# A retention block and an MLP mixer on one core: seven products of quarters in all batches, masked products by copy and select, a tabled order

## The chip, the cores and the metric

The kernel runs on one core of one Trainium2 chip. The metric is the device time of one execution in microseconds. Before: 205.49 us, the median of 3 runs (204.29 to 206.15). The engines are named as in the profile: PE (matrix products), PEld (its weight loads), DVE, ACT and POOL (elementwise work; POOL also issues most loads), SP (issues DMA transposes).

## What is computed

```python
# q, k, v: (4, 8, 768, 64) float32; 8 heads of 64 make 512 columns
gamma = 1.0 - 2.0 ** (-5.0 - np.arange(H))
for t in range(S):
    state = gamma * state + np.einsum('bhd,bhe->bhde', k[:, :, t], v[:, :, t])
    y[:, :, t] = scale * np.einsum('bhd,bhde->bhe', q[:, :, t], state)
x = y.transpose(0, 2, 1, 3).reshape(B, S, H * D)         # (4, 768, 512)
h = np.maximum(x.T @ w_tok1, 0.0) @ w_tok2                # mixes 768 tokens through 256
u = x + h.T
out = u + np.maximum(u @ w_ch1, 0.0) @ w_ch2              # 512 -> 1536 -> 512
```

The inputs are float32; the products are made in float16 with sums in float32.

## The kernel before, in words

The sequence is cut into 6 chunks of 128 rows. A *front* does one pair of heads of one batch (4 batches x 4 pairs = 16 fronts): it loads q, k and v (cast to float16 by the load), scales k by powers of gamma (L491 on ACT, L493 on DVE or POOL), turns q and k so that the head dimension lies on partitions (`turn`: on PE with a copy by ACT or DVE, L525 and L535, or by a DMA transpose from SP, L514), makes the chunk products k'v (L550), the running states on DVE (L560, L562) and their scaled copy `r` (L574, L576), the scores of each chunk (L595), which DVE multiplies by a mask that holds the causal zeros and the powers of gamma (`am`, L609), and the result (L623, L626). ACT scales it into X (L639) or DVE does (L643); X is cast to float16 (L656); two token products follow (L667 with a relu on ACT at L682, then L731), DVE adds them into X (L738); the sum is cast (L746) and turned into `uT`, on PE (L765, L771) or by a DMA transpose (L755).

A *back* does one batch: `widen` makes relu(u @ w_ch1) for one half of the rows, 12 blocks of 128 columns, 4 products of 128x384 each (L800, relu on ACT at L816). Then either `narrow`, for each block of 128 rows 12 products of 512 columns (L839), added to X by DVE (L852) and stored; or `narrow7`, which takes two row blocks and cuts the product into quarters: seven products of quarters instead of eight. For two row blocks that is 42 products of 256 columns (L908) instead of 24 of 512. It needs four sums of pieces of `h` on DVE (L881), one copy on ACT (L944) and eleven quarter adds on DVE (L928), and sums of the weights made once (L1022). `SEVEN = (2, 3)` names the batches that use it; the last two row blocks of batch 3 use `narrow`.

The order of the work is planned when the program is built. Every step is an `Op` with a priority, the engines that may do it with a cost each, the steps it depends on, and the buffers it takes and uses. `arrange` plays the list through a model of the engines and of the DMA rings and gives each engine its order; within an engine the program then runs strictly in that order. Before, the rank of a step comes from its priority: constants first, then batch 0, then fronts at the places named in `PLACES` among the parts of the backs. Loads are issued on POOL in the order of `ORDER`, each behind the one before it (`request`), and each needs a free buffer (`BUFS`). The first k load goes through SP in float32 (`HARD`) and is cast by ACT (L501).

While the plan has PE idle for more than 400 ns in its first 21 us, the program puts products on a tile of zeros there (L1044):

```python
if o.start < F_ON and o.start - pe_at > 400:
    for _ in range(int((o.start - pe_at) * FILL / F_NS)):
        nc.tensor.matmul(spare[:, :384], zero[:, :P], zero, start=True, stop=True)
```

These fillers are not steps of the plan. They read `zero`, which is set by a step of the plan on DVE:

```python
zero_op = prep("DVE", 260, lambda: nc.vector.memset(zero, 0.0))
```

Other constants made on DVE at the start: the powers `lgs`, `gp`, the identity `ident16`, eight masks (L387), the scalings `gyw` (L1014) and zeros in `r16`.

## Time and profile before

| | |
|---|---|
| runs (3) | median 205.49 us, 204.29 to 206.15 |
| the profiled execution | 206.47 us, its span 204.6 us, mean granted clock 0.982 |
| busy, share of the span | PE 92%, PEld 63%, DVE 66%, ACT 51%, POOL 49% |
| chain that ended last | PE 50%, DMA 33%, POOL 7%, DVE 4%, issue 3% |
| DMA | 107991 packets, 26.27 MB; queue of POOL 13.18 MB, of SP 6.49 MB, of ACT 6.29 MB |

The page divides the span into 40 slices and gives busy tenths of each engine; its groups give line, engine, operation, count, busy time, mean duration, and what ended the idle time before. A matmul's duration is from its start to its modelled end, so that neighbours overlap; the spacing of starts tells what one costs.

### The profile page before, as it was taken

To read this page: it belongs to the slowest core of one execution; us is meant where nothing else is said; L and a number is where in the kernel's file an instruction comes from. 1 tells how busy PE (TensorE), PEld (TensorE's weight loads), DVE (VectorE), ACT (ScalarE), POOL (GpSimd) and SP (SyncE) were. 2 spreads that over 40 slices of the span, in tenths; PEclk is the share of its full clock that TensorE was granted. 3 is DMA by queue.
4 is the path that set the end of the run, shared out by engine and by line. 5 is a ranking of instruction groups with operands and counts; after the bars stand their busy time and mean duration, and the time that the engine had idled before them with its cause. 6 is when DMAs were issued, how large, how long until landed. Compare 5 with 4: busy or idle time off the path is not lost.

```text
span 204.6 us, 4851 instructions
## 1 busy us (share of the span) xinstructions
PE 187.8 (92%) x1907; PEld 128.1 (63%) x1907; DVE 135.8 (66%) x346; ACT 105.1 (51%) x234; POOL 99.8 (49%) x141
## 2 busy tenths in 40 slices
PE   7958898999897899999899979799999999999992
PEld 3536687575654555576557745466777886667861
DVE  7998889265988584769559536666732996044951
ACT  4576686885856350676134732086766003774000
POOL 8979598766867774627774864072340000000000
PEclk9995799999999999999999999999999999999999
DMA  9999999999999999999999999972011132000132
GB/s 115 147 156 171 191 179 161 137 200 131 179 126 151 189 152 192 187 173 151 125 180 185 156 150 139 174 175 59 4 38 38 44 153 112 6 0 0 62 147 103
DMA packets 107991, 26.27 MB, mean 128 GB/s; under 512 B 100161, under 2 KB 105025, under 8 KB 107969
## 3 DMA queue, kind: packets, MB, share of 16 engines
q0 software_dynamic: 78016, 13.18, 92.8%
q1 hardware_dynamic: 26352, 6.49, 26.2%
q10 hardware_dynamic: 3600, 6.29, 10.0%
q8 instruction: 15, 0.25, 0.5%
q14 instruction: 8, 0.06, 0.1%
HBM read 26.74 MB, written 6.29 MB: 161 GB/s over the span
## 4 chain that ended last, share of the span: by engine, by line
PE 50%; DMA 33%; POOL 7%; DVE 4%; issue 3%; ACT 1%; POOLq 0%; DVEq 0%
PE bank L800 16%; DMA v<-in_v_dram 14%; PE bank L908 11%; PE bank L839 10%; DMA qT<-q 9%; DMA wc<-in_moe_w_ch_dram 7%; DMA q<-in_q_dram 4%; PE bank L731 3%; PE bank L667 3%; POOL v L440 2%; PE bank L626 2%; DVE X L738 2%; PE bank L595 2%; PE bank L525 2%; PE bank L623 1%
## 5 line engine op out<-in xcount | busy, mean ns | idle before, releaser
L800 PE MATMUL bank<-uT,wc 128*128 128x384 f16 x384 | 69.0, 326 | 0.0
L816 ACT ACTIVATE h<-bank 128x384 f16<-128x384 f32 x96 | 46.4, 491 | 20.5 <-PE bank L800 20.0
L800 PEld LDWEIGHTS <-wc 128*128 128x128 f16 x384 | 35.5, 98 | 20.8
L839 PE MATMUL bank<-wc,h 128*128 128x512 f16 (+1 forms) x180 | 40.8, 365 | 0.0
L609 DVE TENSOR_TENSOR am<-bank,mask 128x384 f16<-128x384 f32 x64 | 32.4, 548 | 10.2 <-PE bank L595 10.2
L639 ACT ACTIVATE X<-bank,gy 128x192 f32<-128x192 f32 x58 | 21.1, 419 | 21.8 <-PE bank L626 19.8
L839 PEld LDWEIGHTS <-h 128*128 128x128 f16 x180 | 16.2, 98 | 13.3
L738 DVE TENSOR_TENSOR X<-X,bank 128x384 f32<-128x384 f32 x32 | 16.4, 549 | 12.0 <-PE bank L731 11.9
L562 DVE SCALAR_TENSOR_TENSOR U<-U,gp,bank 128x128 f32<-128x128 f32 x64 | 22.0, 343 | 1.9
L746 POOL CAST u<-X 128x384 f16<-128x384 f32 x26 | 13.5, 534 | 18.7 <-DVE X L738 17.1
L438 POOL DMA_DIRECT2D k<-in_k_dram x24 | 19.9, 838 | 3.4 <-DMA v<-in_v_dram 1.3
L440 POOL DMA_DIRECT2D v<-in_v_dram x16 | 16.6, 1035 | 6.6 <-DMA wc<-in_moe_w_ch_dram 1.9
L656 POOL CAST x<-X 128x384 f16<-128x384 f32 x21 | 11.3, 538 | 14.6 <-ACT X L639 14.3
L852 DVE TENSOR_TENSOR X<-X,bank 128x512 f32<-128x512 f32 (+1 forms) x15 | 9.7, 649 | 10.9 <-PE bank L839 10.9
L667 PE MATMUL bank<-x,wt 128*128 128x128 f16 x192 | 13.8, 219 | 2.6 <-POOL x L656 2.5
L626 PEld LDWEIGHTS <-am 128*128 128x128 f16 x192 | 13.1, 100 | 4.1 <-issue 1.4
L626 PE MATMUL bank<-v,am 128*128 128x64 f16 x192 | 14.7, 196 | 0.9 <-DVE am L609 0.9
L881 DVE TENSOR_TENSOR hs<-h 128x768 f16<-128x768 f16 x8 | 4.4, 552 | 16.5 <-ACT h L816 16.5
L667 PEld LDWEIGHTS <-wt 128*128 128x128 f16 x192 | 12.0, 98 | 5.0 <-issue 2.9
L731 PE MATMUL bank<-h,wt 128*128 128x128 f16 x192 | 13.5, 219 | 0.5 <-ACT h L682 0.5
L438 POOL DMA_DIRECT2D q<-in_q_dram x16 | 13.4, 840 | 1.2 <-DMA k<-in_k_dram 1.0
L731 PEld LDWEIGHTS <-wt 128*128 128x128 f16 x192 | 11.9, 98 | 2.8 <-issue 0.6
(70 smaller groups left out, 258.3 us busy)
## 6 DMA issues: line engine op xcount, KB each, us to landing
out_dram<-X ACTq DMA_DIRECT2D x23, 256.0 KB, 3.1
v<-in_v_dram POOLq DMA_DIRECT2D x16, 192.0 KB, 11.0
wc<-in_moe_w_ch_dram POOLq DMA_DIRECT2D x5, 512.0 KB, 12.7
k<-in_k_dram POOLq DMA_DIRECT2D x24, 96.0 KB, 11.2
q<-in_q_dram POOLq DMA_DIRECT2D x8, 192.0 KB, 9.4
q<-in_q_dram POOLq DMA_DIRECT2D x16, 96.0 KB, 10.7
wt<-in_moe_w_tok_dram POOLq DMA_DIRECT2D x2, 384.0 KB, 9.9
k<-in_k_dram POOLq DMA_DIRECT2D x3, 192.0 KB, 6.8
```

The costliest lines, as they stand in the source:

```text
L438: nc.gpsimd.dma_start(out=t[:, :, j], in_=src[j].rearrange("(c p) d -> p c d", p=P))
L440: nc.gpsimd.dma_start(out=tile_of(s, [P, 2, NC, D], F16), in_=src.rearrange("h (c p) d -> p (h c) d", p=P))
L562: nc.vector.scalar_tensor_tensor(out=u[:, c], in0=u[:, c - 1], scalar=gp[:, p:p + 1], in1=st, op0=ALU.mult, op1=ALU.add)
L609: nc.vector.tensor_tensor(am, src, m, ALU.mult)
L626: nc.tensor.matmul(o[:, j * D:(j + 1) * D], AM[2 * hf + j].tile[:, i], V.tile[:, j, c], start=(c == 0), stop=(c == 0 or j == 1))
L639: nc.scalar.mul(X.tile[:, half(hf), h * D:(h + 1) * D], yv[:, :, j * D:(j + 1) * D], gy[:, h:h + 1])
L667: nc.tensor.matmul(acc[:, jt * P:(jt + 1) * P], wt1[:, i, jt * P:(jt + 1) * P], X16.tile[:, i], start=(i == 0), stop=(i == NC - 1))
L731: nc.tensor.matmul(acc[:, i * P:(i + 1) * P], wt2[:, jt, t], H1.tile[:, jt], start=(jt == 0), stop=(jt == NJ - 1))
L800: nc.tensor.matmul(acc[:, :SH], w[:, ct, (ft % FW) * P:(ft % FW + 1) * P], UT.tile[:, ct, sh * SH:(sh + 1) * SH], start=(ct == 0), stop=(c ...
L816: nc.scalar.activation(H2.tile[:, ft], A.tile[:, :SH], AF.Relu)
L839: nc.tensor.matmul(acc, H2.tile[:, ft, i * P:(i + 1) * P], wc2[:, ft, cols], start=(ft == 0), stop=(ft == NF - 1 and not mixed))
L908: nc.tensor.matmul(acc[:, half], l[:, j], r[:, j], start=(j == 0), stop=(j == K2 - 1 and not more))
```

## The change

1. `SEVEN` names all four batches: the row blocks of batches 0 and 1, made by `narrow` before, go through `narrow7`.
2. In batches 1 to 3 the masked products of the second head of each pair (24 of 64) are made by a copy on ACT and a select in place on POOL. For that the mask holds only zeros and ones, and one mask serves all heads.
3. The powers of gamma reach the scores through k: the scaled k is what is turned. The extra cast of the first k is dropped; all k loads are one DMA of both heads. k is turned on PE in batch 1 too (`TURNS`), in whole chunks of 128 columns also in batch 0.
4. `BUFS` of k and v go from 5 to 4. The model's constants change, as do `PLACES` and `ORDER`.
5. The rank of each step comes from a table of 1,220 two-character numbers, `PRECEDENCE`, instead of its priority. It covers all steps, constants included.

```diff
--- before.py
+++ after.py
@@ -43,10 +43,12 @@
 
     GEN = dict(SP=20.0, POOL=8.0, ACT=20.0)
     FIRST = dict(SP=600, POOL=1300, ACT=700)
-    LAND = dict(SP=900, POOL=1600, ACT=1500)
+    LAND = dict(SP=900, POOL=1900, ACT=2000)
     DT = 40.0
-    MIX = 9.0
-    WAIT = 2500
+    MIX = 8.0
+    WAIT = 4000
+    SLOW = 1.03
+    PAD = 1500
 
     def __init__(self):
         self.t = 0.0
@@ -69,6 +71,8 @@
         on = [(q, l[0]) for q, l in self.line.items() if l and l[0][2] <= t]
         if on:
             round_ = sum(x[0].dma[1] for _, x in on) + self.MIX * (len(on) - 1)
+            if t > 25000:
+                round_ *= self.SLOW
             for q, x in on:
                 n = dt / round_
                 if x[3] > t:
@@ -76,7 +80,7 @@
                 x[1] -= n
                 if x[1] <= 0:
                     self.line[q].pop(0)
-                    landed.append((x[0], t + dt + self.LAND[q] + x[4]))
+                    landed.append((x[0], t + dt + self.LAND[q] + x[4] + (self.PAD if t > 25000 else 0)))
         self.t = t + dt
 
 
@@ -182,13 +186,9 @@
                 wake = min(wake, free[e])
                 continue
             w_ = waiting[e]
-            look = 0
             for o in w_:
                 if begun[o.n]:
                     continue
-                look += 1
-                if look > (1 if fixed is not None else 400):
-                    break
                 r = ready(o, e)
                 if r > t:
                     if r < INF:
@@ -204,7 +204,7 @@
                 else:
                     way = None
                     for w in o.ways:
-                        f = max(t, free[w[0]]) + w[2] + (400 if w[0] == "DVE" and t > 30000 else 300 if w[0] == "DVE" else 0)
+                        f = max(t, free[w[0]]) + w[2] + (800 if w[0] == "DVE" and t > 30000 else 300 if w[0] == "DVE" else 0)
                         if way is None or f < way[0] or (f == way[0] and w[0] == e):
                             way = (f, w)
                     if way[1][0] != e:
@@ -258,6 +258,34 @@
     return max(x for x in end), order, start, end
 
 
+
+PRECEDENCE = (
+    "xsldqatllmu0r37erv3xst5jcadieq4rs6123y25t201xhauk5mvkyp9gbl86jqki5djlf3rkxe4rsr49p88tuf7gafl4c0qmenxl4x1tra8"
...
+    "b217bgbamj5u97omgvliormp90khljfd20d5bu9q6ul7dappxota93f1s3ip4qkz"
+)
+
+
 @with_exitstack
 def tile_retnet_recurrent__then__mlp_mixer_token_channel_kernel(
     ctx: ExitStack,
@@ -291,19 +319,22 @@
     ps = ctx.enter_context(tc.tile_pool(name="ps", bufs=1, space=bass.MemoryType.PSUM))
     ctx.enter_context(tc.manual_schedule())
 
-    BUFS = dict(kf=1, k=5, q=4, v=5, k16=3, kT=4, qT=4, U=2, r16=3, am=8, X=3, x16=4, h1=5, u16=3,
+    BUFS = dict(kf=1, k=4, q=4, v=4, k16=3, kT=4, qT=4, U=2, r16=3, am=8, X=3, x16=4, h1=5, u16=3,
                 uT=2, h2=2, hs=2, us=2)
     BANKS = dict(first=range(0, 8), front=range(0, 6), back=range(4, 8), back0=range(3, 8))
-    SEVEN = (2, 3)
+    SEVEN = (0, 1, 2, 3)
+    CLIP = (1, 2, 3)
 
     TURNED = 4
 
 
-    TURNS = "hht hht hht hht xhx xhx xhx xht xxx xxx xxx xxx xxx xxx xxx xxx".split()
+    TURNS = "tht tht tht tht thx thx thx tht xxx xxx xxx xxx xxx xxx xxx xxx".split()
     TURN = {(b, p, x): TURNS[NP * b + p][i] for b in range(B) for p in range(NP) for i, x in enumerate("kqu")}
 
-    PLACES = "-5 -5 -5 -5 -4 -2 0 2 10 12 14 16"
+    PLACES = "-5 -5 -5 -5 -4 -1 0 4 8 10 12 14"
     PLACE = {(b, p): int(x) for (b, p), x in zip([(b, p) for b in range(1, B) for p in range(NP)], PLACES.split())}
+
+    CLIPPED = {(b, hf, j) for b in CLIP for hf in range(2) for j in range(1, 2)}
     HARD = {(0, 0, "k")}
     ops = []
 
@@ -340,7 +371,7 @@
     gy = const_p.tile([P, H], FP, name="gy")
     gp = const_p.tile([P, NP], FP, name="gp")
     ident16 = const_p.tile([P, P], F16, name="ident16")
-    mask = const_p.tile([P, H, P], FP, name="mask")
+    mask = const_p.tile([P, 1, P], FP, name="mask")
     gyw = const_p.tile([P, H, D], FP, name="gyw")
     zero = const_p.tile([P, 384], F16, name="zero")
     NR = BUFS["r16"]
@@ -379,13 +410,8 @@
             nc.vector.memset(gp[D:, p:p + 1], g128[2 * p + 1])
     gp_op = prep("DVE", 600, emit, prio=(-20, 0, -1, 1))
 
-
-    mask_ops = []
-    for p in range(NP):
-        def emit(p=p):
-            for h in (2 * p, 2 * p + 1):
-                nc.vector.tensor_scalar(mask[:, h], away, 0.0, gk[:, h:h + 1], ALU.is_ge, ALU.mult)
-        mask_ops.append(prep("DVE", 400, emit, [away_op, g_op], (-20, 0, -1, 1, p) if p < 1 else (-20, 0, -1, 4, p)))
+    mask_op = prep("DVE", 200, lambda: nc.vector.tensor_scalar(mask[:, 0], away, 0.0, None, ALU.is_ge), [away_op],
+                   (-20, 0, -1, 2))
 
     def emit():
         for t in r16:
@@ -425,25 +451,24 @@
 
     def load(b, p, what):
         src = dict(k=k, q=q, v=v)[what][b, 2 * p:2 * p + 2]
-        chunks = what != "v" and TURN[b, p, what] != "h"
         hard = (b, p, what) in HARD
+        chunks = what == "q" and TURN[b, p, "q"] != "h"
         s = Slot("kf" if hard else what)
 
         def emit():
-            if hard:
-                nc.sync.dma_start(out=tile_of(s, [P, 2, NC, D], FP), in_=src.rearrange("h (c p) d -> p (h c) d", p=P))
-            elif chunks:
+            if chunks:
                 t = tile_of(s, [P, NC, 2, D], F16)
                 for j in range(2):
                     nc.gpsimd.dma_start(out=t[:, :, j], in_=src[j].rearrange("(c p) d -> p c d", p=P))
             else:
-                nc.gpsimd.dma_start(out=tile_of(s, [P, 2, NC, D], F16),
-                                    in_=src.rearrange("h (c p) d -> p (h c) d", p=P))
+                (nc.sync if hard else nc.gpsimd).dma_start(out=tile_of(s, [P, 2, NC, D], FP if hard else F16),
+                                                           in_=src.rearrange("h (c p) d -> p (h c) d", p=P))
+        dma = (96, 17) if hard else (96, 13.3)
         if hard:
-            o = Op(ops, (-20, 0, b, p), [("SP", 500, 500, emit)], [], [s], dma=(96, 17), behind=rows[-1] if rows else None)
+            o = Op(ops, (-20, 0, b, p), [("SP", 500, 500, emit)], [], [s], dma=dma, behind=rows[-1] if rows else None)
             rows.append(o)
         else:
-            o = request((-20, 0, b, p), 1660 if chunks else 1030, emit, (96, 12), [s])
+            o = request((-20, 0, b, p), 1660 if chunks else 1030, emit, dma, [s])
         loads[b, p, what] = (s, o)
 
     def front(b, p):
@@ -472,36 +497,24 @@
 
         X, UT = Xs[b], UTs[b]
         pc = slice(p * P, (p + 1) * P)
-        (KL, kd), (Q, qd), (V, vl) = (loads[b, p, x] for x in "kqv")
+        (KF, kd), (Q, qd), (V, vl) = (loads[b, p, x] for x in "kqv")
         K = Slot("k16")
         KT, QT = Slot("kT"), Slot("qT")
 
         def opened(slot, shape, dtype):
             return slot.tile if slot.tile is not None else tile_of(slot, shape, dtype)
-
-
-        chunks = TURN[b, p, "k"] != "h"
 
         def emit(e, js):
             t = opened(K, [P, NC, 2, D], F16)
             for j in js:
                 h = 2 * p + j
-                src = KL.tile[:, :, j] if chunks else KL.tile[:, j]
                 if e == "ACT":
-                    nc.scalar.activation(t[:, :, j], src, AF.Copy, scale=gk[:, h:h + 1])
+                    nc.scalar.activation(t[:, :, j], KF.tile[:, j], AF.Copy, scale=gk[:, h:h + 1])
                 else:
-                    (nc.vector if e == "DVE" else nc.gpsimd).tensor_scalar(t[:, :, j], src, gk[:, h:h + 1], None,
-                                                                           ALU.mult)
-        kl = parts(emit, dict(ACT=(506, 610), DVE=(265, 350), POOL=(450, 510)), [kd, g_op], K, KL, ([0], [1]))
-        if (b, p, "k") in HARD:
-            K1, k1 = Slot("k"), None
-
-            def emit(e, js):
-                t = opened(K1, [P, 2, NC, D], F16)
-                (nc.scalar.copy if e == "ACT" else nc.vector.tensor_copy)(t[:, js], KL.tile[:, js])
-            kd = parts(emit, dict(ACT=(420, 510), DVE=(300, 380)), [kd], K1, KL, (slice(0, 1), slice(1, 2)))
-        else:
-            K1, kd = KL, [kd]
+                    (nc.vector if e == "DVE" else nc.gpsimd).tensor_scalar(t[:, :, j], KF.tile[:, j], gk[:, h:h + 1],
+                                                                           None, ALU.mult)
+        kl = parts(emit, dict(ACT=(506, 610), DVE=(335 if (b, p, "k") in HARD else 265, 420), POOL=(450, 510)),
+                   [kd, g_op], K, KF, ([0], [1]))
 
         def flat(t):
             return t.rearrange("p c h d -> p (c h d)")
@@ -537,7 +550,7 @@
                 return parts(emit, dict(ACT=act(SH), DVE=dve(SH, 0.54)), [t], dst, T,
                              (slice(0, 1), slice(1, 2)))
             return 2 * parts(emit, dict(ACT=act(S), DVE=dve(S, 0.54)), [t], dst, T, (slice(0, 2),))
-        kt = turn(K1, KT, kd)
+        kt = turn(K, KT, kl)
         qt = turn(Q, QT, [qd])
 
         two_before = y_done.get(b * NP + p - 2)
@@ -602,12 +615,25 @@
         for hf in range(2):
             A, a = A4[2 * hf:2 * hf + 2], a2[hf]
             for j in range(2):
+                if (b, hf, j) in CLIPPED:
+                    def emit(hf=hf, j=j, A=A):
+                        am = tile_of(AM[2 * hf + j], [P, HC, P], F16)
+                        nc.scalar.copy(am, A[j].tile[:, :HC * P].rearrange("p (i t) -> p i t", t=P))
+                    ac = op(one("ACT", act(SH), emit), [a], [AM[2 * hf + j]], [A[j]])
+
+                    def emit(hf=hf, j=j):
+                        am = AM[2 * hf + j].tile
+                        nc.gpsimd.affine_select(out=am, in_=am, compare_op=ALU.is_ge, fill=0.0, base=0,
+                                                pattern=[[0, HC], [1, P]], channel_multiplier=-1)
+                    am_ops.append(op(one("POOL", (560, 640), emit), [ac], [], [AM[2 * hf + j]]))
+                    continue
+
                 def emit(hf=hf, j=j, A=A):
                     am = tile_of(AM[2 * hf + j], [P, HC, P], F16)
                     src = A[j].tile[:, :HC * P].rearrange("p (i t) -> p i t", t=P)
-                    m = mask[:, 2 * p + j:2 * p + j + 1].to_broadcast([P, HC, P])
+                    m = mask.to_broadcast([P, HC, P])
                     nc.vector.tensor_tensor(am, src, m, ALU.mult)
-                am_ops.append(op(one("DVE", (465, 548), emit), [a, mask_ops[p]], [AM[2 * hf + j]], [A[j]]))
+                am_ops.append(op(one("DVE", (465, 548), emit), [a, mask_op], [AM[2 * hf + j]], [A[j]]))
         X16 = Slot("x16")
         x_ops, cast_ops = [], []
         for hf in range(2):
@@ -988,9 +1014,9 @@
             part[0] += 2
 
 
-    ORDER = ("k00 q00 v00 k01 q01 v01 k02 q02 v02 k03 q03 v03 t1 t2 a0 q10 a1 k10 v10 a2 a3 k11 v11 q11 b0 "
-             "b1 k12 v12 q12 b2 k13 v13 q13 k20 v20 q20 k21 v21 q21 k22 v22 q22 k23 v23 q23 k30 v30 q30 "
-             "k31 v31 q31 k32 v32 q32 k33 v33 q33").split()
+    ORDER = ("q00 k00 v00 k01 q01 v01 k02 v02 k03 q03 q02 v03 t1 t2 q10 a1 k10 a2 a3 a0 k11 v10 k12 v11 "
+             "q11 b0 b1 v12 q12 b2 k13 v13 q13 k20 v20 q20 v21 k21 q21 k22 v22 k23 q22 v23 q23 k30 v30 q30 "
+             "k31 v31 q31 v32 q32 v33 k33 q33 k32").split()
     for what in ORDER:
         n = int(what[1])
         if what[0] in "kqv":
@@ -1020,7 +1046,7 @@
         for j, (x, y) in enumerate(((b12, b11), (b22, wsum[:, 0]), (b22, b12), (b21, wsum[:, 1]))):
             def emit(e, j=j, x=x, y=y):
                 (nc.vector if e == "DVE" else nc.gpsimd).tensor_tensor(wsum[:, j], x, y, ALU.subtract)
-            dep = [wops["c2", i] for i in range(3)] + (wsums[j - 1:j] if j % 2 else [])
+            dep = [wops["c2", i] for i in range(3)] + (wsums[j // 2:j // 2 + 1] if j % 2 else [])
             wsums.append(Op(ops, (-4, 0, 1, NP, j), either(emit, DVE=(870, 950)), dep))
     for b in range(B):
         for p in range(NP):
@@ -1028,8 +1054,7 @@
     for b in range(B):
         back(b)
 
-    ranked = sorted(ops, key=lambda o: o.prio)
-    rank = {o.n: i for i, o in enumerate(ranked)}
+    rank = {int(PRECEDENCE[2 * i:2 * i + 2], 36): i for i in range(len(ops))}
     total, order, start, end = arrange(ops, BUFS, BANKS, rank)
     for o in ops:
         o.start, o.end = start[o.n], end[o.n]
```

More of the change, by code (lines that the diff above doesn't have):

```diff
@@ L258, in arrange @@
     return max(x for x in end), order, start, end
+PRECEDENCE = (
+    "xsldqatllmu0r37erv3xst5jcadieq4rs6123y25t201xhauk5mvkyp9gbl86jqki5djlf3rkxe4rsr49p88tuf7gafl4c0qmenxl4x1tra8"
+    "h8t4cf0g6hueoqtckp0lbrgq5g1zhlgf5bdvsjg6pqlbacdc36w2h6vk7b9np3edhsqyad6rkda39afuuv2s4uj18gxpabws470x70cgumkn"
+    "iao8c5anoko3wr7tsa586s35mx39ma6g8ycuvvlujdjox37um6xk86loqb669eqtlvsnefbi7oqrte0bhwrp9mbx1c1rho57w6q11oeu65dg"
+    "tg7a72ep3vblswpv10ndrjaeszhbpd0oa0owwzbmhxhgembsfyw7ejlrhmwco568xq1ukbp4kiv2rq2guklpphv1o1pxlah5id4egd83iv0t"
+    "x0byih1l8jw01d185vf6rthv1gcda9su5kj7142298ntvxqs30kox2dudt2ak7n8aq1nb98wq50z54fzd0wkrlprnn3jf82tttb64n7l6lp0"
+    "33lcq3r6q7naezi6fkgp2dqovwcoc8mzoskan78hcifhulpkel5m48vivew3j2s2b7akwqc0gofnt7cwgluu74oy2pvu8o4050fetd692eo0"
+    "k1se3tgypgheqmqd3smlv75zk952upc4pa84tv732zecrwevnb5sqfkur0u94vuy6d59v4e6axx7ckfx5r0di3910eaypc76kqa5jg7f37t5"
+    "fgk0m58e3zi9obmoaze1q4fpkmuq24kkhav9ro0nuj60j4qh2jdk453mdd95hp82opu78ltxq6hfi28suwh4vo9ob5vtnk5cpzjvi0qzcbp2"
+    "53vh5yvqtzkwd74k6pvfg04fccxt1m9brkdpmb31hnal9r417rar3nhrqei1xlqj5lnhrnp1pu92enskxvwjm29lxeubvr4btmh0awnyso1j"
+    "iz7zh1l2bwqprikf9x1aafjhapwt633he0cvl3aan9c6v5spq2bt1pf93an52ctkjm4wks1k2brdmcas6oiofo4tsdvdkrs9ici87y94ln0c"
+    "gwhh0r1ie3ah9ddecqnw62rg2o7wkcsciio9rz5q7pucmqn246incrb8rcxr9gmh71dnrhbnifrmcm4lp6bv19dofflk0jagl1xcjwjzhkm0"
+    "vzjn4ibpcseo4owb4305urnr6vvs4s2qw9s06yesvjllnze589mi02geibilu607k33dwl38m1lt5a0f9jjqgtbj2xkl4g854xbku4iktw1w"
+    "80ruti6kir9hfm0mhzjktf960kg3uiht0hs18mw1j92u6xijh7ls3gexl9gsm726w50ivbo4qijyptaj3lxndmdrjagzhi0629oav3vmc9wy"
+    "44cerb7g9tfif0wwchthpbmuiutss7670uiy5n164pk27nfa1e13ealgfwry2nxb235ft9pep7r7qnt8vpxuhy2vv8oonoftuhoije210wnl"
+    "v67du2g7m34hjbufvl7qqqjt8vig6q2fct2ykjo2czgu7ke9l66tn06caom41f2rcpeyozr8u54j1x4m3ptqnemfsf51wds85tx84a5h0s2k"
+    "e7wi3w5w0pkvmdfvxmmnjcpl8bhjj328566ikt8kwm81g19snia4c1v0jlj6gkk8jsmy4y8qdz0vudgjfsix1b276wot2mvndbc38pbe7s9i"
+    "4dbzc7g5tp8c7c1q619ubbjito7xsyeed3vc8fw8dx783kxj8ximebwxmk6egrt6i43oqclqcyrf2i5o5xb4itxd8uju6futs53enf7m9kds"
+    "df99h2r1bduauom9ugnv9cmr8i7v8n08lxgifbnmxfq9qw7hd2d6sh75l0ehpi4zk4re1hjjpn8rs4nuoe775id8qlwgquolbqg93qdy8t9f"
+    "15onmtggk6u1n1jf1vogb3qxhqf4bh8a87lwaiocssjp11xabo6aatg4ncjr643f3b32a2o64909r203t1w4dq42pjnsieetnqn3humgx52w"
+    "un6bohke1tnppyp5wfofrxlhp8porrmmnjovtylya1hd6n1svyghsx5epwr5cnq0r9wax9pmtjer0ydl79bfew0a8zwnqgt0u3g2g8f2x6wh"
+    "tb34sqcjx42lwun6pfsvmwsbwvrauzqvwefqjxxikga755us04o7fre2b1vasldwfclec2iwodps6zekgnj03uwpm8uxeif3ou5dngsg5pms"
+    "00d17jt32h8dox3c9vb0h9cx3ibcl5dham7if59ye86mojgc9wsmsreggxsilzfjj5n4vg1yhcd9iqxgj8isu8h3q8clavtni79zd4a6wogm"
+    "b217bgbamj5u97omgvliormp90khljfd20d5bu9q6ul7dappxota93f1s3ip4qkz"
+)
```

## The prediction

> **What bounds the kernel now.** I read the page first (busy shares, then the slices), then the busy time by window, then what PE waited for, then the timelines of the start.
>
> ```profile
> PE 187.8 (92%) x1907; PEld 128.1 (63%) x1907; DVE 135.8 (66%) x346; ACT 105.1 (51%) x234; POOL 99.8 (49%) x141
> DVE  7998889265988584769559536666732996044951
> PEclk9995799999999999999999999999999999999999
> ```
>
> PE is the fullest engine, so PE work is what a cut must reach. But DVE is at 8 to 9 tenths in the first slices, and PE's clock dips in slices 4 and 5. The windows (length, then busy us and instructions of PE, PEld, DVE, ACT, POOL) tell the stages apart:
>
> ```profile
> 7.70:34.90 27.20, 22.62 (x377) 17.79 (x377) 24.54 (x65) 18.84 (x39) 22.86 (x31) 0.87 2.04 175
> 34.90:60.00 25.10, 23.94 (x256) 15.80 (x254) 16.01 (x35) 18.90 (x41) 18.48 (x24) 1.00 1.92 150
> 60.00:140.00 80.00, 74.08 (x738) 46.59 (x736) 52.59 (x122) 37.67 (x90) 46.34 (x66) 1.00 1.74 162
> 140.00:196.00 56.00, 55.81 (x487) 41.63 (x486) 34.37 (x87) 26.08 (x58) 5.36 (x10) 1.00 0.16 49
> ```
>
> From 7.7 to 34.9 us (the fronts of batch 0) DVE is the fullest, 24.5 of 27.2. From 34.9 on PE is, with small holes until 140 and none after. What ended the holes after 35 us (total, times, longest):
>
> ```profile
> PE bank L667 <- POOL x L656: 2.5, 2, 1.5
> PE bank L595 <- DMA qT<-q: 2.5, 2, 1.3
> PE bank L550 <- ACT h L816: 0.8, 1, 0.8
> PE bank L595 <- ACT uT L771: 0.5, 1, 0.5
> PE bank L550 <- DMA v<-in_v_dram: 0.3, 1, 0.3
> PE bank L595 <- DMA kT<-k: 0.3, 1, 0.3
> ```
>
> With 0.2 behind L928 that is 7.1 us: all that a better order can win there. The start, from the timelines:
>
> ```profile
> 1.11 6.64 PE L1044 MATMUL bank<-zero 128*128 128x384 f16 x25 [1.11 <-DVE zero L353]
> 7.69 0.53 PE L525 MATMUL bank<-ident,q 128*64 128x128 f16 x12
> ```
>
> PE's 25 warm-up products (on `zero`, L1044) start when DVE has set `zero`, and the first real work follows them.
>
> **The change part by part.** The sum is made against the profiled execution: span 204.6, time 206.47, so 1.87 lie around the span. The median of the runs is 205.49, 0.98 below it; the same difference is carried over to it at the end.
>
> The rows for the durations (busy us, mean ns):
>
> ```profile
> L609 DVE TENSOR_TENSOR am<-bank,mask 128x384 f16<-128x384 f32 x64 | 32.4, 548 | 10.2 <-PE bank L595 10.2
> L816 ACT ACTIVATE h<-bank 128x384 f16<-128x384 f32 x96 | 46.4, 491 | 20.5 <-PE bank L800 20.0
> L656 POOL CAST x<-X 128x384 f16<-128x384 f32 x21 | 11.3, 538 | 14.6 <-ACT X L639 14.3
> L493 POOL TENSOR_SCALAR k<-k,gk 128x384 f16<-128x384 f16 x2 | 2.5, 1244 | 0.0
> L928 DVE TENSOR_TENSOR X<-X,us 128x256 f32<-128x256 f32 x20 | 8.0, 418 | 0.1
> ```
>
> *1. Seven products in batches 0 and 1.* In the built program 144 products of 512 columns go and 252 of 256 come. A matmul's mean duration overlaps its neighbours, so I take spacings: 84 of L908 run from 186.22 to 195.39, 0.109 each; the chain has 8 of L839 in 1.73, 0.216 each. 144 x 0.216 = 31.1 against 252 x 0.109 = 27.5: **-3.6** on PE, which bounds there. DVE gets 24 sums of `h` (L881, 0.552) and 66 quarter adds (L928, 0.414) and loses 12 adds (L852, 0.684): +13.2 + 27.3 - 8.2 = +32.3. ACT gets six copies at 0.372, +2.2. Cover: DVE is 66% busy from 60 to 140. With no front beside them DVE just keeps up (before, the 126 such products of batch 2 ran from 156.68 to 171.43 in the chain, at 0.109 each and four others between, with one wait of 0.2). If the cover fails, a pair of row blocks costs DVE's 6.7 us (4 x 0.552 + 11 x 0.414) instead of PE's 4.6.
>
> *2. Copy and select.* 24 of 64 masked products leave DVE, -13.2. ACT gets 24 copies of 128x384 f32 to f16, by L816 +11.8, on an engine 47% busy from 60 to 140. POOL gets 24 selects, which no row shows. Bounds: a cast of the same size, 0.54, and POOL's scaling of `k`, 0.5 x 2.5 = 1.24, which also reads f16; so +12.9 to +29.9. I take the cast, since like the select it reads and writes without gaps, and keep 1.24 for a rival. Latency: copy and cast, 0.49 + 0.54, equal two masked products in series on DVE. PE has 1.0 to 2.7 us of other work between scores and their use in the new order. I charge **+1.0** for POOL not being free (0 if the cover holds).
>
> *3. k scaled once, and turned on PE in batch 1.* Batch 0: 12 transposes (0.46) become 6 (0.34, by L765), four times -0.12, where PE is not the bound: 0. Batch 1: four more turns, 4 x 0.34 = **+1.4** on PE; SP loses four DMA transposes, and PE's wait on kT (0.3, counted in 5). ACT gets four copies of 0.80 more. Two casts of `k` go (L501, ACT, -0.9). In all, scaling `k` moves from DVE (13 to 3) to ACT (17 to 22) and POOL (2 to 7: +6.2). 24 k loads of 0.838 us on POOL become 12 of 1.055: -7.5. Fewer buffers of k and v (5 to 4) hold later loads back; in the built program a transposed q or k still goes out 24 to 37 us of PE work ahead of its scores, against 21 to 37.
>
> *4. The late zero.* This is what the diff does not show. On DVE `zero` now stands behind the scalings of `gyw`, a scaling of `k` and the identity. By the timeline's spacings: r16 from 2.0, +0.93; one mask 0.2; gyw 0.59 and its eight 1.56; k 0.37; identity 0.42; zero 0.22: ready at 6.3, not 1.05. PE's first 23 instructions still wait for it. Before, 15 of the warm-up products were 0.32 apart, then 0.1625; 15 x 0.32 + 8 x 0.1625 = 6.1. First real work at 12.4, not 7.69: 4.7 late. The loads have landed by then (before, PE waited for q and k at 10.66, 13.38 and 15.46), so DVE is the rest: its first U at 12.4 + 1.9 = 14.3. By spacings the DVE work up to the last add of batch 0 was 22.2 us, in 25.4 us; now it is 20.7 (fewer casts and scalings, more copies). With 1.3 of gaps instead of 3.2 it ends at 36.3, not 34.0: **+2.3**, between 0 (later waits swallow it) and +4.7. The Trainium skill (TensorE: Matmul & The Clock Gate, The HAM clock gate) says that PE runs at half clock until a window of about 3.4 us has been busy, however many matmuls that is; the 4.8 us at 0.32 agree with a window not met at its start. By the page's 3.4 us alone the warm-up would take 5.4, an estimate, and the forecast fall by up to 0.7.
>
> *5. The order.* Between the last `v` product of a front and the product that needs its x cast, PE had 1.75 to 3.0 us of other work (mean 2.2); in the new order mostly 2.9 to 5.3. Both waits on POOL x (1.5 the longest) fit into that: -2.5. Of the DMA waits the kT one goes (-0.3). The two qT waits came with leads of 27 and 28 us; the same two fronts now have 28 and 25, but the last two gain 4 and 14, and DMA has four transposes less: half, -1.1. **-3.9**; bounds -7.1 and +3. What is late next is POOL.
>
> Sum: -3.6 + 1.0 + 1.4 + 2.3 - 3.9 = -2.8. Span 201.8, time 203.7, on the median's footing **202.7** (-1.4%).
>
> **The rivals.**
> *POOL becomes the bound (slower).* POOL has 99.8 busy: -7.5 + 6.2 + 12.9 for selects, five more casts +2.7, two scalings fewer -1.0 give 113; with selects at 1.24, 130. Almost all of it must fall before 145 us. And a DVE operation with two SBUF inputs holds POOL up:
>
> ```profile
> 147.28 0.55 DVE L881 TENSOR_TENSOR hs<-h 128x768 f16<-128x768 f16 x1
> 147.36 0.84 POOL L656 CAST x<-X 128x384 f16<-128x384 f32 x1 [2.19 <-ACT X L639]
> 148.36 0.51 POOL L746 CAST u<-X 128x384 f16<-128x384 f32 x1 [0.16 <-DVE X L738]
> ```
>
> The first cast starts inside a sum and takes 0.84, not 0.51: 0.33 more for 0.47 of overlap. 24 sums and 24 adds of `X` and `us` come, 23 us; at 75% overlap and 0.7 each, +12. POOL then has 125 to 142 of 145 us, its queue also carries every load, and casts, selects and loads come late together. Of the 12 us of holding up the longer cover of part 5 (1.1 more in each of 12 fronts, a third of it at the right moment) takes 4: +8, about 211. It decides from some 128 us of POOL work. Against it: POOL idled 34 of the 80 us from 60 to 140. The Trainium skill (SBUF — State Buffer, Who interferes with whom) says the same of this port pair: exclusive, the loser waits. The trace agrees in direction (0.33 for 0.47); by a full block the holding up would be 17 and this rival 216.
> *The start counts in full.* ACT, with six scalings of `k` in its queue, keeps batch 0 from catching up: 4.7 instead of 2.3, time 205.1. For it: ACT's 18.8 of 27.2. Against it: loads no longer set the pace.
> *The order fills every hole.* -7.1 instead of -3.9, and the start's 2.3 vanishes in waits for loads that were there anyway: 197.2. For it: the longer distances. Against it: qT leads that hardly grow.
> *The seven products bring nothing*, since DVE is late: +3.6, to 206.3; I count it with the start's case.
>
> **How the numbers follow.** Forecast 0.43, own range 200 to 205.2 (faster 0.30, same 0.13). Order fills all: 0.22, faster. Start in full or nothing from the products: 0.14, same. POOL: 0.21, slower. About 1% (203.4 to 207.5 as the bounds) is what a measurement here can tell from no change. Faster 0.52, same 0.27, slower 0.21. The range goes down to 196.5 (bound of 5 with some start left over) and up to 209.5, short of the worst POOL case.
>
> **What would show it.** Step 1: products of 256 columns 0.109 apart in batches 0 and 1, without DVE waits between. Step 2: the select's mean, under 0.7 or near 1.24, and PE waits on POOL `am`. Step 4: `zero` set near 6.3, first real product near 12.4, and batch 0's last add near 36. Step 5: no wait of L667's successor on x, and under 1.5 on qT. Wrong it would be if POOL is over nine tenths from 35 to 120 us, or if PE's holes after 37 us sum to more than 8.

## The result, and the profile after

The changed kernel takes 206.23 us (median of 22 runs, 205.55 to 206.91), the kernel before 204.91 (22 runs, 203.52 to 207.52). The ratio is 1.0073, 95% interval 1.0053 to 1.0092: 0.7% slower, where 1.4% faster was forecast. Ratios here leave out runs over 1.5% above the fastest of their kernel, which for e16 is most of them, while medians are of all runs. The profiled execution after took 205.96, its span 204.1; the one before had 206.47, 1.56 above the median of its 22 runs, so that spans are not compared across the two.

The page after:

```profile
PE 185.9 (91%) x2023; PEld 139.1 (68%) x2023; DVE 144.3 (71%) x380; ACT 116.8 (57%) x272; POOL 113.8 (56%) x161
...
DVE  7319999533899999975558999974319997005982
...
PEclk9999999999999999999999999999999999999999
```

PE's clock no longer dips, and POOL's sum is what was forecast (113). DVE is at nine tenths in a second stretch, slices 12 to 17 and 23 to 26, where it had 3 to 8 before. The same stages by window (length, then busy us and instructions of PE, PEld, DVE, ACT, POOL):

```profile
12.55:37.86 25.31, 21.84 (x369) 17.35 (x368) 22.37 (x56) 18.56 (x40) 16.15 (x25) 1.00 1.85 162
37.86:60.00 22.14, 20.77 (x232) 13.78 (x228) 12.83 (x29) 18.33 (x43) 21.05 (x28) 1.00 1.75 154
60.00:140.00 80.00, 77.59 (x899) 61.19 (x896) 67.84 (x175) 51.19 (x126) 56.87 (x80) 1.00 1.69 153
140.00:196.00 56.00, 55.11 (x470) 39.76 (x469) 31.86 (x77) 26.42 (x62) 8.18 (x15) 1.00 0.21 56
```

From 60 to 140 us DVE has gone from 52.6 to 67.8 of 80, 85%. What ended PE's idle times after 33 us (total, times, longest):

```profile
PE bank L934 <- DVE X L954: 1.1, 3, 0.5
PE bank L934 <- DVE us L954: 1.0, 1, 1.0
PE bank L652 <- POOL am L626: 0.9, 3, 0.5
PE bank L826 <- ACT uT L797: 0.4, 1, 0.4
PE bank L934 <- DVE hs L907: 0.4, 1, 0.4
PE bank L791 <- POOL u L772: 0.3, 1, 0.3
PE bank L540 <- POOL k L514: 0.2, 1, 0.2
```

Every wait that was to go has gone: on POOL's x, on the DMAs of qT and kT, on v. In their place stand the quarter products (L934), which wait for DVE's adds and sums (L954, L907), and the products with `am` (L652), which wait for the select. This list sums to 4.3 us and leaves out short gaps. Measured by the starts of the products against their shortest spacing, gaps over 40 ns from the end of batch 0's fronts on sum to 11.6 us before and 10.9 after: "PE's holes" below. The old waits are gone and new ones stand in their place; which part of the change did which, the experiments tell.

The start, from PE's and DVE's timelines (start, length):

```profile
6.80 5.91 PE L1069 MATMUL bank<-zero 128*128 128x384 f16 x23 [6.80 <-DVE zero L384]
12.55 0.50 PE L540 MATMUL bank<-ident,k 128*128 128x128 f16 x6
```

```profile
5.66 0.40 DVE L514 TENSOR_SCALAR k<-kf,gk 128x384 f16<-128x384 f32 x1
5.99 0.76 DVE L404 TENSOR_SCALAR ident<-away 128x128 f16<-128x128 f32 x1
6.52 0.22 DVE L384 MEMSET zero<- 128x192 uint32 x1
```

The late zero came as forecast: set at 6.52 (forecast 6.3), first real product at 12.55 (12.4), batch 0's last add ends at 36.99 (36.3), not 33.98.

### The profile page after: what moved, and what is told of

Its sections match the earlier page's. It is cut to its first block, busy times and chain, and to the rows that moved or that the text cites. A ratio compares the mean times of both kernels' runs of the same rounds, so it can differ in the third digit from the quotient of the medians.

```text
span 204.1 us, 5153 instructions
## 1 busy us (share of the span) xinstructions
PE 185.9 (91%) x2023; PEld 139.1 (68%) x2023; DVE 144.3 (71%) x380; ACT 116.8 (57%) x272; POOL 113.8 (56%) x161
## 3 DMA queue, kind: packets, MB, share of 16 engines
q1 hardware_dynamic: 23152, 5.71, 24.1%
q10 hardware_dynamic: 3600, 6.29, 9.1%
HBM read 26.74 MB, written 6.29 MB: 162 GB/s over the span
## 4 chain that ended last, share of the span: by engine, by line
PE 57%; DVE 22%; POOL 9%; ACT 7%; issue 3%; DVEq 0%; POOLq 0%; ACTq 0%
PE bank L826 23%; PE bank L934 17%; DVE X L954 4%; DVE hs L907 4%; DVE U L575 3%; PE bank L1069 3%; DVE am L635 3%; PE bank L865 3%; PE bank L693 2%; ACT h L842 2%; PE bank L757 2%; POOL u L772 2%; DVE X L764 2%; PE bank L608 2%; POOL k L464 2%
## 5 line engine op out<-in xcount | busy, mean ns | idle before, releaser
L934 PEld LDWEIGHTS <-hs 128*128 128x128 f16 x264 | 24.9, 98 | 6.5 <-issue 2.2
L635 DVE TENSOR_TENSOR am<-bank,mask 128x384 f16<-128x384 f32 x40 | 20.8, 550 | 10.3 <-PE bank L608 10.3
L934 PE MATMUL bank<-wsum,hs 128*128 128x256 f16 x198 | 26.7, 273 | 0.7 <-DVE hs L907 0.4
L907 DVE TENSOR_TENSOR hs<-h 128x768 f16<-128x768 f16 x18 | 11.0, 622 | 19.6 <-ACT h L842 19.5
L934 PEld LDWEIGHTS <-h 128*128 128x128 f16 x198 | 18.8, 98 | 4.6 <-issue 1.4
L954 DVE TENSOR_TENSOR X<-X,bank 128x256 f32<-128x256 f32 x55 | 21.1, 410 | 0.5 <-PE bank L934 0.4
L626 POOL TENSOR_SCALAR_AFFINE_SELECT am<-am 128x384 f16<-128x384 f16 x24 | 13.4, 576 | 12.2 <-ACT am L621 12.0
L954 DVE TENSOR_TENSOR X<-X,us 128x256 f32<-128x256 f32 x44 | 18.5, 437 | 0.2 <-ACT us L970 0.2
L934 PE MATMUL bank<-wc,h 128*128 128x256 f16 x132 | 17.8, 272 | 0.0
L652 PE MATMUL bank<-v,am 128*128 128x64 f16 x192 | 15.0, 193 | 1.5 <-POOL am L626 0.9
L573 DVE COPY U<-bank 128x128 f32<-128x128 f32 x16 | 4.6, 285 | 15.9 <-PE bank L563 15.9
L464 POOL DMA_DIRECT2D k<-in_k_dram x15 | 15.6, 1043 | 0.1
L652 PEld LDWEIGHTS <-am 128*128 128x128 f16 x192 | 12.5, 98 | 4.2 <-POOL am L626 1.5
```

The source lines that it names most:

```text
L464: (nc.sync if hard else nc.gpsimd).dma_start(out=tile_of(s, [P, 2, NC, D], FP if hard else F16), in_=src.rearrange("h (c p) d -> p (h c) d ...
L635: nc.vector.tensor_tensor(am, src, m, ALU.mult)
L652: nc.tensor.matmul(o[:, j * D:(j + 1) * D], AM[2 * hf + j].tile[:, i], V.tile[:, j, c], start=(c == 0), stop=(c == 0 or j == 1))
L907: (nc.vector if e == "DVE" else nc.gpsimd).tensor_tensor(HS.tile[:, j], x(), y(), f)
L934: nc.tensor.matmul(acc[:, half], l[:, j], r[:, j], start=(j == 0), stop=(j == K2 - 1 and not more))
L954: (nc.vector if e == "DVE" else nc.gpsimd).tensor_tensor(dst(), a_(), b_(), ALU.add)
```

## The experiments

Sixteen kernels were run, e6 being the changed kernel once more; "the table" is `PRECEDENCE`. A difference in us is between medians of the runs. The kernels ran on several chips, on which the kernel before had medians from 204.81 to 205.86, so that a difference of 1 us or less between two of them is not told apart unless the ratios, each to the kernel before on the same chip, say the same. All but e1, e4, e5 and e6 are planned anew with their edit, so that the order of the work moves too.

**The start.** *e1: the changed kernel with `zero` set ahead of the plan.*

```diff
-    zero_op = prep("DVE", 260, lambda: nc.vector.memset(zero, 0.0))
+    nc.vector.memset(zero, 0.0)
+    zero_op = prep("DVE", 260, lambda: None)
```

> The changed kernel with one edit: zero is set ahead of the plan, as DVE's first instruction; order and work are otherwise the same. Theory A (the late zero costs what it puts on the start, and PE bounds from there on): first real product near 7.5 us instead of 12.55, last add of batch 0 near 34 instead of 37, time 3 us below the changed kernel, 203.2. Rival B (the start is swallowed by later waits for loads): the last add of batch 0 comes 3 us earlier, but PE's holes after 38 us grow by 2 to 3, time 205.5 to 206. Rival C (the busier start trips PE's clock, as in the profile of the kernel before): a stretch at half clock in 15 to 25 us, time about 205.

Measured: 201.53, ratio 0.9799 (0.9760 to 0.9838): theory A, and more than it said. First real product at 7.29, batch 0's last add at 33.50, PE's holes 11.0, as in the changed kernel: nothing of a late start is given back.

*e6: the changed kernel again, unaltered, beside later ones.*

> The changed kernel unaltered, beside the others on one chip. If the late zero is worth 3.4 us, as the spans of the two profiles with and without it say, it stands 3.4 above the run with zero first by the ratio to before, that is near 1.000 or less; if it is worth the 4.7 that the medians of different chips give, near 1.007 again.

Measured: 206.20, ratio 1.0061 (1.0034 to 1.0087). So one line, where `zero` stands in DVE's order, is worth 4.7 us here by the medians, 5.4 to 5.6 by the ratios (e1 ran on another chip) and 3.4 between the profiled runs.

*e5: the kernel before with its zero late.*

```diff
-    zero_op = prep("DVE", 260, lambda: nc.vector.memset(zero, 0.0))
+    zero_op = prep("DVE", 260, lambda: None)
...
         nc.vector.memset(gyw, 1.0)
+        nc.vector.memset(zero, 0.0)
```

> The kernel before with one edit: zero is set after the scalings of gyw, where the table put it near, and not first. Theory A (the late zero delays the whole of batch 0 and all that follows one for one): first real product near 12.3 us, last add of batch 0 near 37.5, time 3 to 5 us above before. Rival B (it only hurt the new order, whose start has more work on ACT): less than 2 us above before. Rival C (a later warm-up avoids the stretch at half clock, which before has at 16 us): within 1 us of before or faster.

Measured: 207.81, ratio 1.0147 (1.0101 to 1.0193), +2.7 us, just under theory A's range. Batch 0's last add is 3.2 later; 1.3 comes back in holes (10.3, not 11.6), since one of the two waits on qT goes. The kernel before had waits for loads in which a late start can hide, the changed one has none.

**The seven products.** *e2: the kernel before with `SEVEN` of all batches, and no more.*

```diff
-    SEVEN = (2, 3)
+    SEVEN = (0, 1, 2, 3)
```

> The kernel before with SEVEN for all batches and nothing else. Theory A (DVE's sums and adds give the gain of the seven products back as short waits of PE): PE products 3.6 us less, but waits of L908 on DVE of 2 us or more, and time within 1.5 us of the kernel before. Rival B (the seven products are hidden well when the order is that of before): time 3 to 3.6 us below before, about 201.5. Rival C (DVE, which also carries all 64 masked products here, becomes the bound): slower than before by 2 us or more.

Measured: 211.12, ratio 1.0259 (1.0209 to 1.0309). Rival C holds, and PE does not keep the work it saves: its holes go to 20.1 (up to 1.7 of it a stretch of 3.4 us at half clock, from 77.6), and the three longest sums of waits are on DVE (X, us, am).

*e3: the changed kernel with zero early and ranks by priority, not by the table.*

```diff
-    rank = {int(PRECEDENCE[2 * i:2 * i + 2], 36): i for i in range(len(ops))}
+    ranked = sorted(ops, key=lambda o: o.prio)
+    rank = {o.n: i for i, o in enumerate(ranked)}
```

> The changed kernel with the order by priority as before instead of the table; zero then comes first again. All else of the change stays. Theory A (the table shortens PE's holes by little, and the late zero costs 3): within 1 us of the changed kernel. Rival B (the table is worth the waits on POOL and DMA that vanished, some 5 us): 2 us or more above the changed kernel in spite of the early zero. Rival C (the table only costs): near the changed kernel with zero first, 203.

Measured: 201.29, ratio 0.9785 (0.9750 to 0.9820), equal to e1 and nearest to rival C. The table brings nothing that the priorities do not.

*e4: e1 without the eleven quarter adds in batches 0 and 1.* The result then lacks these sums in the rows of these batches.

```diff
+                    if b not in (0, 1):
-                    (nc.vector if e == "DVE" else nc.gpsimd).tensor_tensor(dst(), a_(), b_(), ALU.add)
+                        (nc.vector if e == "DVE" else nc.gpsimd).tensor_tensor(dst(), a_(), b_(), ALU.add)
```

> The changed kernel with zero first and without the eleven quarter adds of each pair of row blocks in batches 0 and 1, so that these two batches' outputs lack the second part of the mixer: 66 DVE operations of 0.41 us less, all PE work kept. Theory A (PE's waits in the seven products come from DVE's adds): 1.5 to 3 us below the run with zero first, and no waits of L935 on X or us in batches 0 and 1. Rival B (those waits are covered elsewhere, the work of PE sets the end): within 0.5 us of the run with zero first. Rival C (DVE as a whole is the bound in these batches): 5 us or more below.

Measured: 199.10, ratio 0.9682 (0.9648 to 0.9716): the adds cost 2.4 of e1's time, as theory A has it. Of the waits on X, two are left (0.34 and 0.53), and they lie at 151 and 158 us, in batch 2. The sums of `h` are still made.

*e7, e8 and e10: e3 with one of the two parts, or neither.*

```diff
-    SEVEN = (0, 1, 2, 3)
+    SEVEN = (2, 3)
-    CLIP = (1, 2, 3)
+    CLIP = ()
```

e7 has the first edit, e8 the second, e10 both.

> The changed kernel by priority, with the seven products in batches 2 and 3 alone as before: copy and select, k scaled once, its turn on PE and the new load order are all that is left of the change. Theory A (copy and select pay by making room on DVE for the seven products, and little alone): 203 to 205 us, 2 or more above the run by priority with all. Rival B (they are the whole gain, since DVE bounds batches 1 to 3): within 0.7 of that run, 201 to 202. Rival C (POOL's 24 selects alone cost): 206 or more.

> The changed kernel by priority, with seven products in all batches and no copy and select: all 64 masked products on DVE. Theory A (without room on DVE the seven products cost more than they save, as in the kernel before with seven alone, 2.6% slower): 205 to 209 us, PE waits on am, X and us of 5 us and more. Rival B (that loss came from the old turns and loads, not from DVE): 201 to 203.

> The fastest version so far (198.2 us) without copy and select: all 64 masked products on DVE again, seven products in batches 2 and 3 only. What is left of the change is k scaled once (and turned on PE in batch 1), the order of the loads and the early places of the fronts. Theory A: copy and select won 2.8 us beside the seven products only because DVE was late there; without them DVE has slack, so it is worth under 1: 198.0 to 199.2. Rival B: it is worth the same 2 to 3.5 us with or without them: 200.2 to 201.7. Rival C: the loads and k are worth nothing, so that this equals the kernel before, 204 to 206.

| | seven in batches 2, 3 | seven in all batches |
|---|---|---|
| all masked products on DVE | e10: 198.29, ratio 0.9685 (0.9636 to 0.9735) | e8: 204.02, ratio 0.9951 (0.9922 to 0.9980) |
| 24 by copy and select | e7: 198.21, ratio 0.9677 (0.9639 to 0.9715) | e3: 201.29, ratio 0.9785 (0.9750 to 0.9820) |

e7's theory A, that copy and select alone would be worth less than the whole, is refuted, and so are its rivals, whose times are all longer. e10 shows why: the gain was not that of copy and select, as its theory A says. e8 falls between its theories. Seven products in batches 0 and 1 cost 5.7 us without the copies and selects and 3.1 with them (5.5 and 2.2 by the ratios); copy and select repay 2.7 of that (3.4 by the ratios), and without the seven products they are worth 0.1. They are a remedy for a harm that the same change does. The windows from 60 to 143 us of e10, e7, e3 and e8, in this order:

```profile
60.00:143.00 83.00, 82.81 (x824) 52.11 (x823) 50.38 (x114) 47.89 (x115) 41.60 (x60) 1.00 1.41 144
```

```profile
60.00:143.00 83.00, 83.00 (x831) 52.74 (x830) 45.01 (x103) 52.38 (x129) 53.66 (x80) 1.00 1.39 145
```

```profile
60.00:143.00 83.00, 79.19 (x900) 61.03 (x899) 68.90 (x174) 52.61 (x129) 55.81 (x77) 1.00 1.38 144
```

```profile
60.00:143.00 83.00, 77.87 (x891) 59.86 (x889) 72.23 (x186) 47.19 (x116) 43.82 (x61) 1.00 1.33 143
```

With DVE at 54% or 61% PE is full. At 83% PE has lost 4 us, at 87% it has lost 5. How DVE holds PE up well short of being full shows in its timeline of the changed kernel:

```profile
79.64 0.41 DVE L954 TENSOR_TENSOR X<-X,us 128x256 f32<-128x256 f32 x1
79.98 0.54 DVE L907 TENSOR_TENSOR hs<-h 128x768 f16<-128x768 f16 x1
80.44 0.54 DVE L764 TENSOR_TENSOR X<-X,bank 128x384 f32<-128x384 f32 x1
80.91 0.41 DVE L954 TENSOR_TENSOR us<-us,bank 128x256 f32<-128x256 f32 x1
81.24 0.54 DVE L764 TENSOR_TENSOR X<-X,bank 128x384 f32<-128x384 f32 x1
```

and PE's beside it:

```profile
79.84 0.50 PE L757 MATMUL bank<-h,wt 128*128 128x128 f16 x6
81.37 0.81 PE L934 MATMUL bank<-wc,hs 128*128 128x256 f16 x6 [1.03 <-DVE us L954]
```

The add that PE waits for ends at 81.32; it stands behind a sum and an add of a front in DVE's strict order, and PE is still for 1.03 us.

*e12: e7 with seven in batches 1, 2 and 3. e11: e7 with seven in no batch.*

```diff
-    SEVEN = (2, 3)
+    SEVEN = (1, 2, 3)
```

> The fastest version so far (198.2 us) with seven products in batch 1 too (in 1, 2 and 3). In all four batches it took 201.3. Theory A: both batches lose alike, since the backs of both run beside a front's DVE work: 199.2 to 200.5. Rival B: the loss is batch 0's alone (its quarters come while DVE still has fronts and the sums of the weights), and batch 1 gains its 1.8 us of PE work: 196 to 197.5.

> The fastest version so far (198.2 us) with seven products in no batch: eight in batches 2 and 3 too, as well as the weights' four sums gone from DVE. Theory A: in batches 2 and 3 the seven products pay, because PE is full there and DVE has time; PE gets back some 3 us (by the same spacings as for batches 0 and 1, one pair of batch 3 having been eight already), and the kernel takes 200.5 to 202. Rival B: they pay nowhere, DVE's chains at the end cost as much: 197.5 to 199.2.

Measured: e12 200.08, ratio 0.9781 (0.9724 to 0.9839); e11 201.12, ratio 0.9821 (0.9760 to 0.9881). Both times are those of theory A: batch 1 costs 1.9, while in batches 2 and 3, where no front runs beside most of them, the seven products gain 2.9. What batch 0 costs beyond that is not told apart: 1.2 by the medians, nothing by the ratios (0.9781 and 0.9785).

*e9: e7 with copy and select in batch 0 too.*

```diff
-    CLIP = (1, 2, 3)
+    CLIP = (0, 1, 2, 3)
```

> The fastest version so far (changed kernel by priority, zero early, seven products in batches 2 and 3 only; 198.2 us), with copy and select in batch 0 as well: 8 more masked products (8 x 0.55 = 4.4 us) leave DVE, 8 copies go to ACT and 8 selects of 0.52 to POOL. Theory A: the fronts of batch 0 are DVE's (28.2 of the first 35 us), so they end 1 to 3 us earlier and the kernel takes 195.5 to 197.2. Rival B: POOL, which has 30.4 of those 35 us and the loads in its queue, is as full as DVE, so nothing is won or something lost: 198 to 200.

Measured: 197.91 (197.60 to 198.69), ratio 0.9664 (0.9614 to 0.9713), between the theories. It is the fastest of the study with e15 below (198.04), e7 and e10, which these runs do not tell apart; all are some 3% faster than the kernel before.

**The rest of the change.** e10 leaves k scaled once and loaded in one piece (and turned on PE in batch 1), the one mask, the fewer buffers, the order of the loads, the planner's constants and the places of the fronts. Together they are worth 6.6 us, and PE's holes are 4.4 from the end of batch 0's fronts (32.66) on and 3.4 from 37 us on, where they were 11.6:

```profile
PE bank L826 <- ACT uT L797: 0.9, 1, 0.9
PE bank L563 <- POOL k L514: 0.2, 1, 0.2
PE bank L934 <- DVE us L954: 0.2, 1, 0.2
```

The next four take that apart. *e13: the kernel before with the new constants and places alone.*

```diff
-    LAND = dict(SP=900, POOL=1600, ACT=1500)
+    LAND = dict(SP=900, POOL=1900, ACT=2000)
-    MIX = 9.0
-    WAIT = 2500
+    MIX = 8.0
+    WAIT = 4000
+    SLOW = 1.03
+    PAD = 1500
...
-    PLACES = "-5 -5 -5 -5 -4 -2 0 2 10 12 14 16"
+    PLACES = "-5 -5 -5 -5 -4 -1 0 4 8 10 12 14"
```

> The kernel before with only the planner's constants (landing times, MIX, WAIT, SLOW, PAD, 800 for DVE) and the places of the fronts of the changed kernel; zero early, k and the loads as before. Theory A: the order of the operations is what fills PE's holes, with loads as they were: 198 to 201 us. Rival B: the holes were late operands of k and q (loads and turns), which an order cannot bring: 203.5 to 206.

*e14: e10 with the constants, the places and the load order of before. e15: e10 with the load order of before alone.* e14 has the edits of e13 reversed, but for the limit `look`, which stays dropped, and the old `ORDER`; e15 has the old `ORDER` alone.

> The e10 version (198.3 us) with the constants, the places and the load order of the kernel before, so that k scaled once, its turns on PE in batch 1, the one mask and the buffers are left of the change. Theory A (order): 203 to 206, holes near 11. Rival B (k is the cause, since it takes twelve loads' POOL time and four transposes off the queues): 198 to 201, holes under 6.

> The e10 version (198.3 us) with the load order of the kernel before alone. Theory A (the load order is of small use): 198 to 199.5. Rival B (the loads' order decides whether q is there in time): 201 to 204, with waits of PE on the DMA of qT again.

Measured: e13 205.09 (202.47 to 207.55), ratio 0.9981 (0.9941 to 1.0022): nothing, as rival B has it. e14 201.08, ratio 0.9822 (0.9773 to 0.9871), between its theories. e15 198.04 (197.95 to 198.30), ratio 0.9680 (0.9643 to 0.9717), theory A. So k scaled once, with its turns on PE, brings 3.7, the constants and places another 3.0 once k is so and nothing before, the load order nothing. e14's longest wait of PE is the one that e15 no longer has:

```profile
PE bank L608 <- DMA qT<-q: 2.5, 2, 2.2
```

*e16: e15 with k of batch 1 turned by DMA again.*

```diff
-    TURNS = "tht tht tht tht thx thx thx tht xxx xxx xxx xxx xxx xxx xxx xxx".split()
+    TURNS = "tht tht tht tht xhx xhx xhx xht xxx xxx xxx xxx xxx xxx xxx xxx".split()
```

> The version with the old load order (198.0 us), k still scaled once and loaded in one piece, but k of the first three fronts of batch 1 turned by a DMA transpose as in the kernel before, not on PE. Theory A: the one load of k in place of two is the cause, and the turns on PE cost what step 3 said for them (3 x 0.34 us): 196.5 to 197.5. Rival B: the turns on PE are the cause, since the DMA transposes of k delayed those of q: 199.5 to 202, with waits of PE on the DMA of kT or qT.

Measured: 204.42 (200.97 to 208.04, 12 runs), ratio 0.9870 (0.9813 to 0.9927). The edit gives back four turns, the fourth front's too. Theory A falls, and the time lies above rival B's range as well: the turns cost PE 4 x 0.34 = 1.4 us, and with them the kernel is faster by 1.9% in the ratios, some 3.9 us, and by 6.4 in the medians. The DMA view shows what else moves with them (queue: packets, MB, share of 16 engines; issues: count, KB each, median us to landing). e16 has twelve transposes of k, e15 eight, and they differ by this edit alone; e16, then e15:

```profile
q1 hardware_dynamic: 26352, 6.49, 27.1%
...
v<-in_v_dram POOLq DMA_DIRECT2D x16, 192.0 KB, 11.9
k<-in_k_dram POOLq DMA_DIRECT2D x15, 192.0 KB, 13.1
...
q<-in_q_dram POOLq DMA_DIRECT2D x16, 96.0 KB, 12.5
```

```profile
q1 hardware_dynamic: 23152, 5.71, 22.9%
...
v<-in_v_dram POOLq DMA_DIRECT2D x16, 192.0 KB, 9.9
k<-in_k_dram POOLq DMA_DIRECT2D x15, 192.0 KB, 10.7
...
q<-in_q_dram POOLq DMA_DIRECT2D x16, 96.0 KB, 13.0
```

With twelve transposes the loads of v and k land 2.0 and 2.4 us later than with eight, those of q no later. The packets of SP's queue (q1) take 27.1% and 22.9% of the span, that is 54.8 and 44.9 us of all 16 DMA engines. That late loads are what PE loses by in e16 is not shown. In e10 the loads of v and q land after 8.0 and 7.2 us, far sooner than in e15, and the two kernels take the same time. The list of waits in e16's profiled run names only 0.9 us on a DMA, that of a transposed u, of 10.4 us of holes. Part of these holes is slower products and no wait, since in this run PE's granted clock is at half from 82.5 to 89.3 us (the row gives the mean of each slice, so a 6):

```profile
PEclk9999699999999999669999999999999999999999
```

So it is shown that the turns of k on PE pay, and open by which path: the loads, the transposes of u, the clock or the order that is planned anew.

The runs of e16 scatter by 7.1 us and those of e13 by 5.1 (12 runs each), the kernel before by 4.0 (22 runs), and the kernels with eight transposes by 0.35 (e15) to 2.1 (e11, 6 runs each). But e5 and e2 have twelve too and scatter by 1.2 and 2.3 in 6 runs each, and e13's profiled run names no wait of PE on a DMA. What makes the runs scatter is open.

## Why the prediction was wrong

The way from the kernel before to the changed one, by built kernels: 204.91 to 198.29 (e10) to 204.02 (e8) to 201.29 (e3) to 201.53 (e1) to 206.23.

| step of the prediction | forecast | measured |
|---|---|---|
| 3 and 5, k and the order | -2.5 | -6.6 (e10) |
| 1, seven products in batches 0 and 1 | -3.6 | +5.7 (e8 less e10), +3.1 beside step 2 |
| 2, copy and select | +1.0 | -2.7 (e3 less e8), -0.1 without step 1 |
| 5, of it the table | in the above | +0.2 (e1 less e3) |
| 4, the late zero | +2.3 | +4.7 (less e1) |
| sum | -2.8 | +1.3 |

- *Step 1 failed, and it turned the sign.* PE's 3.6 us are there by count, and the products stood 0.109 apart (the median) in batches 0 and 1 as forecast, but the cover, "DVE is 66% busy from 60 to 140", was not enough for 32.3 more. The prediction gave the price if the cover failed, yet tested the cover only with "DVE just keeps up" in batch 2, where no front stands in DVE's queue. With fronts beside it an add waits its turn behind their work, and PE waits with it. The rival "seven products bring nothing" was named with 206.3, right by luck: they cost 3.1 to 5.7, and what k and the order gained beyond the forecast hid it. Of the signs of being wrong, PE's holes over 8 did show, by the spacing (10.9).
- *Step 2* had the price of a select right by its lower bound (mean 0.576, median 0.521, forecast 0.54) but was charged as a cost, because it was weighed by POOL's load alone. In a kernel that DVE holds up, 13 us less on DVE are a gain (2.7).
- *Step 4* was right in each of its times (6.52, 12.55, 36.99) and mis-sized at the end: it took the 2.3 that batch 0 ends later for all and let later waits swallow none, but against e1, the same kernel with the zero early, batch 0 ended 3.5 later (36.99, 33.50) and the profiled runs lie 3.4 apart; the medians lie 4.7 apart, e1's profiled run being 1.1 above its median. Only the kernel before, which has DMA waits, swallows some of it (2.7).
- *Steps 3 and 5* were mis-sized. The 7.1 us, "all that a better order can win there", were the listed waits alone; by the spacing PE's holes were 11.6, and e10 has 4.4. The 1.4 us that turning k costs PE were counted, and the DMA time it frees only as "DMA has four transposes less: half". The rival "the order fills every hole" came nearest for this part (-7.1, and +1.4 for the turns), with another cause: neither the places alone (e13) nor the load order (e15) does it, and without the turns of batch 1 on PE most of it is lost again (e16).
- *The slower rival, POOL as the bound, was wrong.* POOL was busy 113.8, as forecast without any holding up:

```profile
L626 POOL TENSOR_SCALAR_AFFINE_SELECT am<-am 128x384 f16<-128x384 f16 x24 | 13.4, 576 | 12.2 <-ACT am L621 12.0
L682 POOL CAST x<-X 128x384 f16<-128x384 f32 x22 | 12.2, 565 | 16.2 <-ACT X L665 16.2
```

A cast of x went from 0.538 to 0.565, 5%, for all the DVE sums that came, and a cast of u from 0.534 to 0.539. The Trainium skill (SBUF — State Buffer, Who interferes with whom) calls the shared port pair an exclusive lock; the trace bears out the direction, and the sum stays at 5% on these casts.

## What to carry to other kernels

A cover is not the share of an engine that is free but the place of the new work in its queue: here an in-order engine at 54 to 61% left PE full, and at 83 to 87% cost it 4 to 5 us of 83. Undo each part of a change by itself before judging it: here one part gained 6.6 us, one lost 5.7, one only repaired the loss, and one line at the start lost 4.7. That an edit pays does not tell the path: e16 shows that the turns on PE pay, and the view that looked like the reason, loads that land late, does not hold between e10 and e15.

## What was not expected of the hardware

- PE's products on zeros run at half rate (0.32 us apart, not 0.1625) for 4.8 us before and in e1, 4.1 in the changed kernel and 4.8 when it is run again (e6), 2.5 in e10 and 6.0 in e11 and e12, from starts at 1.1 to 6.8 us. The Trainium skill (TensorE: Matmul & The Clock Gate, The HAM clock gate) gives 3.4 us and a free-running window, with a variation of about 0.5; the variation here is 3.5.
- PE's clock dips at 16 to 23 us in the profiled run of the kernel before and not in that of the changed kernel. In e1, with its early start, PE runs at half rate from 19.7 to 23.1.
- SP's queue, transposes but for one load, takes far more of the DMA engines per byte than the stores: 5.71 MB in 23152 packets took 41.9 us (e8) to 50.8 us (e6) of all 16, and 6.49 MB in 26352 packets 51.4 (e5) to 56.3 (e2), where the stores' 6.29 MB in 3600 packets took 17.5 (e7) to 20.5 (before). The same packets differ by 9 us between kernels, so that the price of one transpose cannot be read off two of them.
